# Twelve transposes of the first batch moved from DMA to TensorE, with the whole instruction order laid out anew

## The chip, the cores and the metric

The kernel is one program on one core of a Trainium2 chip. The metric is the time of one execution in microseconds, as the device measures it. The engines are named as the profile names them: PE is TensorE (PEld its weight loads), DVE is VectorE, ACT is ScalarE, POOL is GpSimd, SP is SyncE, which here only issues DMAs.

## The reference

Two things are computed one after the other. First, attention for 8 batches of 8 heads, with 512 local tokens and 32 global tokens of 64 numbers each. A global token looks at all 544 keys; a local token looks at the 32 global keys and at the local keys at most 32 places away. Second, an MLP on all 4,352 resulting tokens:

```python
x = attn_out.transpose(0, 2, 1, 3).reshape(B * S, H * D)     # 4352 x 512
h = x @ w_in                                                  # 512 x 2048
g = np.where(h >= 1, h, np.where(h <= -1, 0.0, (h + 1) ** 2 / 4))
out = (g @ w_out).astype(np.float32)                          # 2048 x 512
```

The two weight matrices arrive as 64-bit floats, 8 MB each.

## The kernel before, in words

Every operand of TensorE is held as two fp16 halves, a high one and a low one that is the difference; a product is three products of halves. The two weight matrices are cut into 16 tiles each. A tile of `w_in` is loaded (step `Lw`), decoded from 64-bit words (`wd`, VectorE for the most part), brought to a common scale that needs eight tiles (`ws`), and split into halves (`wh`); `w_out` goes through `Lo`, `od`, `oh` likewise.

A batch goes through these steps. Keys, queries and values are loaded. `scale_k` finds a scale for the keys; in the first two batches it does so by a Gram matrix on TensorE, 24 products. `prep_k` and `prep_q` split and transpose, `swap_q` exchanges halves by a DMA, `prep_v` splits the values and `prep_w` shifts windows of them by DMAs. For each of four blocks of 128 queries and each of two groups of four heads, `att_q` makes the scores (32 small products), `att_a` the probabilities (VectorE adds the mask and finds the extreme, ScalarE takes the exponential, one engine casts the high half, one subtracts for the low half) and transposes them, `att_b` multiplies them with the values (48 small products). `att_x` divides by the sums (VectorE, tile `small_rc`), casts, subtracts and transposes the block's output. Then the MLP follows in 16 stages of 256 tokens, two to a batch: `moe1` (stages 0 and 1, which are batch 0) or `moe_f` (all later ones) make the hidden values, `act` the activation, `moe2` the output. Two more short MLP stages serve the global tokens.

A transpose of a tile of 128 rows and eight blocks of 128 columns is done by `turn` in one of two ways: as one DMA, which SP issues, or as eight transposes on TensorE into a PSUM bank, which ScalarE or VectorE then copies out:

```python
    def turn(who, o, i):
        if who == "d":
            dma_t(o, i)
            return
        n = i.shape[0]
        t = ps_t.tile([P, 8, P], F16, tag="p", name="turn")
        for c in range(8):
            nc.tensor.transpose(t[:, c, :n], i[:, c * P:(c + 1) * P], ident[:n, :n])
        (nc.scalar.copy if who == "a" else nc.vector.tensor_copy)(o, t[:, :, :n])
```

Which way is taken stands in the string `T["turns"]`, 23 letters for a batch: 6 for keys, 5 for queries, 8 for probabilities, 4 for attention outputs. There are letters for batch 0 alone; every later batch uses the DMA. Other strings of `T` choose engines: `casts` and `subs` for the high and low half of the probabilities, `lows` for the low half of an attention output, `glow` for that of an activation, `queues` the issuing queue of each plain DMA (`s` is SP, `a` is ScalarE).

No scheduler orders the instructions. The functions are recorded first and cut into some 4,400 pieces, each of one engine; the table `ORDER` says in which order the pieces are issued, so it sets each engine's own order, and `SLOTS` says which buffer each tile takes. The semaphores follow from the data and the buffers. Every engine works strictly in its order: a piece that waits holds up all that stand behind it on that engine. Nearly all instructions carry the line of the loop that issues them (L1345, L1348 for DMAs on ScalarE's queue, L1350 for DMAs on SP's), so rows are told apart by their tiles: `room` holds most working tiles, `bank` is PSUM, `weights_w` the weights, `twin` the raw `w_out` and later combined weights, `keys_kt` the transposed keys.

Of the kernel before, what the change touches and what calls it, by code (L numbers as in the profile page):

```python
# [131 lines left out]
def attention_moe(nc, memory, q_l, k_l, v_l, q_g, k_g, v_g, w_in, w_out, out):  # L132
# [1137 lines left out]
    for _, _, fn, a in sorted(steps.values(), key=lambda x: x[:2]):  # L1270
# [8 lines left out]

SLOTS = {  # L1280
# [27 lines left out]
}  # L1308

T = dict(es="nnnn", gramq="aaaaaaaa", dg="vvvvvvaaaaavvav", sid="vvvvv", fast=2, grams="ppaaaaaa", sqs="maamaa", cb=200, cbs=5, lk0=4.19,  # L1310
         lq0=1.76, lv0=12, sk=12, sq=14, subs="pppvpppppvppppvppvpvpvpppvpppvvvppppvvvpppppvppvvppvvpppvppvvvpv",
         glow="vpvpppvpvpppppvvvppppppvvppppvvpvppvvppppvvpppvvpppvpppvppppvpppppppvvpvvpppvvpppppvvvvvpppvvpvvvvpvpvppppvvvpppvvpvvvvvpvvvppvppppppppppppppppp",
         turns="aaaaaaaaaaadddddddddddd", casts="vavavvvaavvvvavvvvvvvvaavaavvaaavvaavaaavaaaavaavvavvaaavvvaavav",
         mags="aapapvpaappvppppppapapaaaaapaaaa", lowx="pppppppvpvpvpvpvppppvpvvpppvpppvpvvvpppppvvppppp",
         lows="vvpvvpppppppppppvppppppppppppppp", halves="aaaaaahaabacadacceccacdbidffcbdf", shifts="vavvaaavvvvaaavvvvvavvvvvaaavvvv",
         splits="wpvpwwpvwwvpvvvw", att=1.35, s0=60, s1=100, s2=254.09, wd0=4, wds=2.06, wd8=19.2, wdt=1.9, wh=1.5, whs=1.4, od=58.2,
         ods=2.2, oh=0.7, ohs=0.92, e0=25.78, e1=70, e2=120, e3=156, w0=24.7, w1=24.34, w2=25.15, w3=25.51, z1=18.29, lq1=24, lv2=24.36,
         sv=24.5, sqb=35.02, pk2=20.4, pk3=30, pk4=45.8, pq2=28.03, pq4=44, pv=35.24, pvs=0.33, lw=0.54, lo=32.46, los=2.12, mk=8, mks=2,
         queues="aaaasaaassaaaaassasaassssssaaasaasaaaaaaaasasaaasssassasssasasaasssassasaasaaaaaassassssaasasaaaasaassaaaaaaaaaaaaaasasassasaaaaasssasasssassassaassssasassaaaaaaasssassasaaaaasaaaasaaasaaasaaassasssasaaasssaaaassaaaassaaasssasaassssaaaassaaaaaaasssssssssasssssaasasaaassaasssaasassaaasssassasasaassasaasaasasssaaaassaasasasasaasssaassssasaaasassasssaassssssaasassasassssasssssasasaaaassaasassasaassssasssasaaasasasasaaasasasasaaasaasaaaasssaassasaaasasasaaaaaasasaaasssaasasaaaassssasassasasaasssaassaasaaasssassasaasssaassaasssssssssasssaassassasasassaaasssasasssasssassasasa")
# [66 lines left out]
```

## Time and profile before

| | |
|---|---|
| median of 3 runs | 975.25 us (972.88 to 977.69) |
| the profiled execution | 969.92 us |
| its span, first to last instruction | 968.1 us |
| PE busy | 849.6 us (88%) |
| DVE busy | 764.6 us (79%) |
| ACT busy | 640.7 us (66%) |
| POOL busy | 312.8 us (32%) |

The span lies 1.8 us under its own execution's time, and that execution lies 5.3 us under the median. Busy shares are means over a start in which little can be computed yet and a long middle in which PE hardly rests, so they are to be read by stretch.

### The profile page before, as it was taken

The numbers are of one execution on the slowest core, as the hardware profiler recorded it, in microseconds if no ns is written. First come the engines' busy times: TensorE is split into PE (matmuls) and PEld (weight loads), VectorE is DVE, ScalarE is ACT, GpSimd is POOL, SyncE is SP. The second block draws the span as 40 slices with busy tenths as digits, with TensorE's granted clock in tenths as the row PEclk, the third lists the DMA queues.
The fourth block names the chain that finished last, engine by engine and source line by source line (L and its number), as shares of the span: only waits on it lengthen the run. The fifth ranks groups of instructions, "written<-read, shape, count | busy, mean of one in ns | idle before, by whom it ended". The sixth has DMA issues, their size and how long they took to land.

```text
span 968.1 us, 34765 instructions
## 1 busy us (share of the span) xinstructions
PE 849.6 (88%) x14284; PEld 608.4 (63%) x14284; DVE 764.6 (79%) x2014; ACT 640.7 (66%) x1581; POOL 312.8 (32%) x343
## 2 busy tenths in 40 slices
PE   0464888998898989998899999999899999999998
PEld 0242675856776675767576757676686677677953
DVE  0788998999788887798788797688899888766861
ACT  1386686869786776677586785768686767455540
POOL 2235345234222422531244320533222324234030
PEclk9996899999999999999999999999999999999999
DMA  9977988899989999898988799978998795755101
GB/s 243 239 145 168 209 162 158 134 181 176 153 148 193 168 173 149 152 168 156 164 148 152 137 166 143 158 152 160 173 160 171 145 162 95 132 81 82 48 1 44
DMA packets 392383, 144.10 MB, mean 149 GB/s; under 512 B 361248, under 2 KB 370464, under 8 KB 392224
## 3 DMA queue, kind: packets, MB, share of 16 engines
q1 hardware_dynamic: 305248, 95.37, 58.2%
q10 hardware_dynamic: 86976, 46.52, 22.9%
q8 instruction: 112, 1.84, 0.8%
q14 instruction: 47, 0.39, 0.2%
HBM read 49.81 MB, written 8.91 MB: 61 GB/s over the span
## 4 chain that ended last, share of the span: by engine, by line
PE 28%; DVE 20%; DMA 16%; ACT 10%; issue 6%; POOL 3%; SPq 2%; ACTq 1%; DVEq 0%; POOLq 0%
PE bank L1345 28%; DVE room L1345 12%; DMA room<-room 11%; ACT room L1345 8%; DVE bank L1345 3%; POOL room L1345 3%; ACT junk_junka L1345 2%; DMA keys_kt<-room 1%; DMA room<-in_v_l_dram 1%; ACTq L1348 1%; DVE batch_small_ms L1345 1%; DMA room<-in_v_g_dram 1%; SPq L1345 1%; SPq L1350 1%; DVE small_nb L1345 1%
## 5 line engine op out<-in xcount | busy, mean ns | idle before, releaser
L1345 POOL TENSOR_TENSOR room<-room,room 128x512 f16<-128x512 f32 (+3 forms) x221 | 244.8, 1120 | 532.1 <-ACT room L1345 407.3
L1345 PEld LDWEIGHTS <-room 128*32 128x32 f16 (+1 forms) x7464 | 241.9, 97 | 244.5 <-issue 38.7
L1345 PE MATMUL bank<-weights_w,room 128*128 128x512 f16 x1632 | 372.9, 381 | 7.1 <-POOL room L1345 2.4
L1345 PEld LDWEIGHTS <-weights_w 128*128 128x128 f16 (+1 forms) x3968 | 222.5, 99 | 63.6 <-DVE weights_w L1345 37.3
L1345 PE MATMUL bank<-room,weights_w 128*128 128x128 f16 (+1 forms) x3840 | 222.8, 217 | 7.4 <-ACT room L1345 3.1
L1345 ACT CAST room<-room 128x512 f16<-128x512 f32 (+1 forms) x238 | 136.1, 586 | 83.5 <-DVE room L1345 59.0
L1345 PE MATMUL bank<-room,twin 128*128 128x128 f16 (+1 forms) x2304 | 131.1, 216 | 12.1 <-DMA room<-room 9.6
L1345 PEld LDWEIGHTS <-twin 128*128 128x128 f16 x2304 | 124.6, 98 | 18.6 <-DMA room<-room 9.0
L1345 ACT ACTIVATE room<-room,small_nb 128x128 f32<-128x128 f32 x256 | 100.4, 394 | 40.8 <-DVE small_nb L1345 25.2
L1345 ACT ACTIVATE room<-bank,batch_small_ms 128x512 f32<-128x512 f32 (+1 forms) x112 | 82.8, 749 | 37.4 <-DVE bank L1345 20.0
L1345 DVE SCALAR_TENSOR_TENSOR bank<-bank,batch_small_ms,room 128x512 f32<-128x512 f32 (+1 forms) x112 | 80.4, 723 | 19.8 <-ACT room L1345 19.5
L1345 ACT ACTIVATE junk_junka<-room 128x512 f16<-128x512 f32 (+2 forms) x124 | 77.5, 625 | 14.0 <-DMA room<-in_k_l_dram 2.8
L1345 DVE TENSOR_TENSOR room<-room,room 128x512 f16<-128x512 f32 (+1 forms) x97 | 75.3, 780 | 10.1 <-ACT room L1345 9.8
L1345 DVE CUSTOM_DVE_ANT_0 room<-bank,const_mask,batch_small_q 128x128 f32<-128x128 f32 x256 | 73.8, 345 | 11.7 <-PE bank L1345 9.8
L1345 DVE SCALAR_TENSOR_TENSOR room<-room,batch_small_ms,bank 128x512 f32<-128x512 f32 (+1 forms) x112 | 79.1, 713 | 1.3
L1345 ACT COPY room<-bank 128x512 f32<-128x512 f32 (+2 forms) x100 | 55.5, 571 | 29.4 <-PE bank L1345 15.0
L1345 DVE SCALAR_TENSOR_TENSOR room<-room,batch_small_ms,room 128x512 f32<-128x512 f32 (+1 forms) x64 | 49.8, 780 | 6.9 <-ACT room L1345 5.1
L1345 DVE TENSOR_TENSOR bank<-bank,room 128x512 f32<-128x512 f32 (+1 forms) x64 | 42.2, 659 | 16.6 <-PE bank L1345 7.2
L1345 PE MATMUL bank<-keys_kt,room 128*32 128x128 f16 x2048 | 40.6, 221 | 10.7 <-DMA room<-room 6.9
L1345 ACT ACTIVATION_READ_ACCUMULATOR room<-room,small_nb 128x1 f32 x256 | 48.6, 190 | 0.0
L1345 PE MATMUL bank<-room,room 128*32 128x64 f16 x3072 | 35.7, 197 | 14.0 <-DMA room<-room 10.5
L1345 PE MATMUL bank<-weights_w 128*128 128x128 bf16 x128 | 15.2, 266 | 35.5 <-DVE weights_w L1345 35.5
(167 smaller groups left out, 916.3 us busy)
## 6 DMA issues: line engine op xcount, KB each, us to landing
room<-room ACTq DMA_DIRECT2D x80, 128.0 KB, 3.7
room<-room SPq DMA_DIRECT2D x64, 128.0 KB, 5.1
weights_w<-in_moe_w_in_dram ACTq DMA_DIRECT2D x25, 256.0 KB, 5.1
twin<-in_moe_w_out_dram ACTq DMA_DIRECT2D x23, 256.0 KB, 5.2
out_dram<-room SPq DMA_DIRECT2D x21, 256.0 KB, 2.9
room<-in_q_l_dram ACTq DMA_DIRECT2D x18, 256.0 KB, 4.2
room<-in_v_l_dram SPq DMA_DIRECT2D x23, 192.0 KB, 4.1
room<-in_k_l_dram ACTq DMA_DIRECT2D x22, 192.0 KB, 5.3
```

Of the source, the lines that this page charges most:

```text
L1345: getattr(getattr(tc.nc, engine), op)(*a, **k)
L1348: tc.nc.scalar.dma_start(*a)
L1350: r = tc.nc.sync.dma_start(*a)
```

## The change

The last twelve letters of `turns` change from `d` to `v` (8 transposes of probabilities) and `a` (4 transposes of attention outputs): in batch 0 these twelve tiles are now transposed by TensorE, and VectorE or ScalarE copies them out of PSUM. The strings `subs`, `glow`, `casts`, `lows`, `lowx` and `queues` hold other letters, and `ORDER` and the large lines of `SLOTS` are other tables of nearly the same length (12 pieces more in `ORDER`). No arithmetic changes.

```diff
-ORDER = ("7 14 5 4 3 16 11 10 17 88 36 40 15 35 152 153 0 1 ...
+ORDER = ("9 8 61 62 63 40 193 64 0 298 66 41 38 39 3 29 27  ...
-    "small.amk": "1 1 0 0 1 0 1 0",
+    "small.amk": "0 0 1 0 1 0 0 1",
-         lq0=1.76, lv0=12, sk=12, sq=14, subs="pppvpppppvppppvppvpvpvpppvpppvvvppppvvvpppppvppvvppvvpppvppvvvpv",
-         glow="vpvpppvpvpppppvvvppppppvvppppvvpvppvvppppvvpppvvpppvpppvppppvpppppppvvpvvpppvvpppppvvvvvpppvvpvvvvpvpvppppvvvpppvvpvvvvvpvvvppvppppppppppppppppp",
-         turns="aaaaaaaaaaadddddddddddd", casts="vavavvvaavvvvavvvvvvvvaavaavvaaavvaavaaavaaaavaavvavvaaavvvaavav",
-         mags="aapapvpaappvppppppapapaaaaapaaaa", lowx="pppppppvpvpvpvpvppppvpvvpppvpppvpvvvpppppvvppppp",
-         lows="vvpvvpppppppppppvppppppppppppppp", halves="aaaaaahaabacadacceccacdbidffcbdf", shifts="vavvaaavvvvaaavvvvvavvvvvaaavvvv",
+         lq0=1.76, lv0=12, sk=12, sq=14, subs="ppppppvppvppvpppppppvpvppvppvppppvvvvvpppvppvppppvpppvvvpppvpvpp",
+         glow="ppppvvpppvpppvppppvvppvppvpvvppvpppppvpvppvpppvvppppvvvppvvpvvvpppvpvvpvppppvppvppvpvpvpppppppvvpvpppppvppppvvvvpvppvpvvpppvppvvpppppppppppppppp",
+         turns="aaaaaaaaaaavvvvvvvvaaaa", casts="aaaaaavvaaaavvvvvvvaavavaaavvvaaavvaaaaaavaavvvvvaaaavvaavavaaav",
+         mags="aapapvpaappvppppppapapaaaaapaaaa", lowx="ppppppppvpvvpppvppppppvpvpppvpvvvppvvpvppppvpvpp",
+         lows="ppppvpppppppvpppppvpvpppvpppvpvp", halves="aaaaaahaabacadacceccacdbidffcbdf", shifts="vavvaaavvvvaaavvvvvavvvvvaaavvvv",
```

VectorE, the first rows of the program. `weights_w_0_69`, `_75`, `_72`, `_67` and `_68` are tiles of `w_in` in decoding; `small_amk` belongs to the scale of the first batch's keys, which lie in `room_94` to `room_99`. Before:

```order
L1345 TENSOR_SCALAR weights_w_0_75<-weights_w_0_75 128x512
L1345 SCALAR_TENSOR_TENSOR bank_123<-bank_123,weights_w_0_75 128x512
L1345 TENSOR_SCALAR room_119<-weights_w_0_72 128x512
L1345 SCALAR_TENSOR_TENSOR weights_w_0_75<-weights_w_0_75,bank_123 128x512
L1345 TENSOR_SCALAR weights_w_0_69<-weights_w_0_69 128x512
L1345 TENSOR_SCALAR weights_w_0_67<-weights_w_0_67 128x512
L1345 SCALAR_TENSOR_TENSOR bank_101<-room_102,weights_w_0_69 128x512
L1345 SCALAR_TENSOR_TENSOR weights_w_0_69<-weights_w_0_69,bank_101 128x512
L1345 SCALAR_TENSOR_TENSOR bank_92<-bank_92,weights_w_0_67 128x512
L1345 SCALAR_TENSOR_TENSOR weights_w_0_67<-weights_w_0_67,bank_92 128x512
```

Now:

```order
L1345 TENSOR_SCALAR weights_w_0_69<-weights_w_0_69 128x512
L1345 SCALAR_TENSOR_TENSOR bank_101<-room_102,weights_w_0_69 128x512
L1345 SCALAR_TENSOR_TENSOR weights_w_0_69<-weights_w_0_69,bank_101 128x512
L1345 MEMSET const_ones_84 128x128
L1345 TENSOR_REDUCE small_amk_106<-bank_107 128x1
L1345 TENSOR_SCALAR small_amk_106<-small_amk_106 128x1 x2
L1345 TENSOR_SCALAR small_dg_108<-const_negid_85,small_amk_106 128x128
L1345 TENSOR_REDUCE small_amk_106<-bank_109 128x1
L1345 TENSOR_SCALAR batch_small_sk_110<-small_amk_106 128x1
L1345 RECIPROCAL batch_small_sk_110<-batch_small_sk_110 128x1
L1345 TENSOR_SCALAR room_155<-room_98,batch_small_sk_110 128x8x64
L1345 TENSOR_SCALAR room_156<-room_99,batch_small_sk_110 96x8x64
```

The scale of the keys stood behind 44 rows, of which the decoding of eight tiles and their common scale; it now stands behind the decoding of one tile and the setting of a constant.

VectorE around the division of the first attention output (the `TENSOR_TENSOR` with `small_rc`). Before:

```order
L1345 CAST room_116<-room_134 128x512
L1345 SCALAR_TENSOR_TENSOR bank_93<-room_133,twin_150 128x512
L1345 TENSOR_SCALAR twin_163<-twin_163 128x512
L1345 TENSOR_SCALAR room_121<-room_98,batch_small_sk_108 128x8x64
L1345 TENSOR_TENSOR room_142<-bank_127,small_rc_158 128x512
L1345 SCALAR_TENSOR_TENSOR room_121<-room_98,batch_small_sk_108,room_121 128x8x64
L1345 TENSOR_SCALAR small_den_157<-small_sum_154 128x8
L1345 TENSOR_SCALAR batch_small_ms_164<-batch_small_ms_164 128x1 x2
L1345 RECIPROCAL batch_small_ms_164<-batch_small_ms_164 128x1
```

Now (a `COPY` of 128x1024 takes transposed probabilities out of a bank):

```order
L1345 COPY room_119<-bank_92 128x1024
L1345 TENSOR_SCALAR twin_157<-twin_157 128x512
L1345 SCALAR_TENSOR_TENSOR bank_92<-room_99,twin_160 128x512
L1345 COPY room_104<-bank_101 128x1024
L1345 COPY room_144<-bank_93 128x1024
L1345 SCALAR_TENSOR_TENSOR weights_w_0_70<-twin_160,bank_92 128x512
L1345 TENSOR_TENSOR room_113<-bank_107,small_rc_162 128x512
L1345 TENSOR_SCALAR twin_150<-twin_150 128x512
L1345 COPY room_99<-bank_92 128x1024
```

Four copies out of PSUM stand ahead of the division now (three are shown), and a fifth behind it.

SP, where batch 0 is transposed. Before:

```order
L1345 DMA_TRANSPOSE room_105<-room_94 128x8x128
L1345 DMA_TRANSPOSE room_125<-room_135 128x8x128
L1350 DMA room_88<-room_112 64x1024
L1350 DMA room_136<-room_118 64x1024
L1350 DMA twin_153<-in_moe_w_out_dram 128x512
L1350 DMA room_119<-room_144 32x1024
L1350 DMA room_119<-room_111 96x1024
L1345 DMA_TRANSPOSE room_125<-room_116 128x8x128
L1345 DMA_TRANSPOSE room_105<-room_126 128x8x128
L1350 DMA qg_qgb_160<-qg_qga_159 64x256
L1345 DMA_TRANSPOSE room_102<-room_104 128x8x128
```

Now, at the same place of the queue:

```order
L1350 DMA room_125<-in_v_g_dram 32x8x64
L1350 DMA twin_160<-in_moe_w_out_dram 128x512
L1350 DMA room_120<-room_133 64x1024
L1350 DMA twin_147<-in_moe_w_out_dram 128x512
L1350 DMA twin_163<-in_moe_w_out_dram 128x512
L1350 DMA room_154<-in_k_l_dram 96x8x64
L1350 DMA room_156<-room_133 32x1024
L1350 DMA room_120<-room_155 64x1024
L1350 DMA room_156<-room_155 96x1024
L1350 DMA room_118<-room_155 64x1024
```

The transposes are gone, and plain DMAs stand closer together.

## Rows read from the trace of the kernel before

**Rows 1.** Windows: length; PE, PEld, DVE, ACT, POOL busy (instructions); clock, DMA, GB/s.
```profile
0.00:52.00 52.00, 13.76 (x84) 9.00 (x85) 20.62 (x50) 14.89 (x26) 11.76 (x37) 1.00 1.12 239
52.00:111.00 59.00, 35.96 (x491) 20.37 (x491) 52.31 (x161) 45.03 (x103) 27.86 (x35) 0.78 0.74 164
111.00:160.00 49.00, 43.08 (x758) 34.22 (x756) 46.17 (x120) 33.20 (x81) 24.34 (x25) 0.96 0.82 175
160.00:260.00 100.00, 90.91 (x1704) 67.89 (x1703) 89.96 (x259) 76.97 (x199) 34.26 (x34) 1.00 0.98 163
260.00:860.00 600.00, 562.10 (x9797) 405.28 (x9795) 493.19 (x1309) 428.68 (x1090) 191.32 (x189) 0.99 0.88 152
860.00:968.10 108.10, 103.80 (x1463) 71.67 (x1459) 62.30 (x121) 41.97 (x87) 23.26 (x26) 1.00 0.26 52
```

**Rows 2.** What TensorE waited for, 0 to 110 us (waits; total us, times, longest).
```profile
PE bank L1345 <- DVE weights_w L1345: 36.5, 8, 18.9
...
PE bank L1345 <- DMA room<-room: 3.1, 1, 3.1
```

**Rows 3.** What VectorE waited for, 0 to 111 us (waits).
```profile
DVE weights_w L1345 <- DMA weights_w<-in_moe_w_in_dram: 22.6, 2, 16.6
DVE small_amk L1345 <- PE bank L1345: 6.5, 2, 6.2
```

**Rows 4.** Busy time from 0 to 100.3 us (windows).
```profile
0.00:100.30 100.30, 41.54 (x419) 24.30 (x420) 62.71 (x172) 51.27 (x113) 35.73 (x68) 0.89 0.91 199
```

**Rows 5.** Timeline of VectorE at the start (start us, us; idle before).
```profile
16.56 0.43 DVE L1345 TENSOR_SCALAR weights_w<-weights_w 128x512 int32<-128x512 int32 x1 [16.56 <-DMA weights_w<-in_moe_w_in_dram]
...
51.25 0.29 DVE L1345 TENSOR_REDUCE small_amk<-bank 128x1 f32<-128x128 f32 x1 [6.17 <-PE bank L1345]
```

**Rows 6.** Timeline of TensorE: Gram matrix of the keys; one turn on TensorE.
```profile
49.03 2.18 PE L1345 MATMUL bank<-room 128*128 128x128 bf16 x24
...
101.80 0.61 PE L1345 MATMUL bank<-const_ident,room 128*128 128x128 f16 x8
```

**Rows 7.** Timeline of 100 to 111 us, from attention output to first hidden product.
```profile
100.32 0.68 DVE L1345 TENSOR_TENSOR room<-bank,small_rc 128x512 f32<-128x512 f32 x1
...
104.24 0.69 DVE L1345 TENSOR_TENSOR room<-room,room 128x512 f16<-128x512 f32 x1 [0.26 <-ACT room L1345]
...
109.91 1.89 PE L1345 MATMUL bank<-room,weights_w 128*128 128x128 f16 x16
```

**Rows 8.** Groups by line and form (busy us, mean ns of one).
```profile
L1345 POOL TENSOR_TENSOR room<-room,room 128x512 f16<-128x512 f32 x150 | 190.3, 1277 | 476.5 <-ACT room L1345 379.4 <-DVE room L1345 46.6 <-issue 18.4
...
L1345 ACT CAST room<-room 128x512 f16<-128x512 f32 x208 | 125.1, 613 | 77.6 <-DVE room L1345 53.8 <-POOL room L1345 4.3 <-issue 3.6
...
L1345 DVE TENSOR_TENSOR room<-room,room 128x512 f16<-128x512 f32 x92 | 71.4, 780 | 10.1 <-ACT room L1345 9.8
...
L1345 DVE TENSOR_TENSOR bank<-bank,room 128x512 f32<-128x512 f32 x56 | 38.7, 692 | 14.6 <-PE bank L1345 5.4 <-ACT junk_junka L1345 4.9 <-ACT room L1345 4.2
...
L1345 DVE CAST room<-room 128x512 f16<-128x512 f32 x34 | 14.7, 440 | 1.9 <-ACT room L1345 1.8
...
L1345 PE MATMUL bank<-const_ident,room 128*128 128x128 f16 x72 | 7.1, 259 | 2.6 <-DVE room L1345 1.8 <-ACT keys_kt L1345 0.7
...
L1345 ACT COPY keys_kt<-bank 128x1024 f16<-128x1024 f16 x5 | 5.0, 1004 | 2.4 <-PE bank L1345 2.4
...
L1345 DVE TENSOR_TENSOR bank<-bank,room 128x256 f32<-128x256 f32 x8 | 3.4, 426 | 2.0 <-PE bank L1345 1.8 <-ACT room L1345 0.2
```

**Rows 9.** DMA issues (KB each, median us from issue to landing).
```profile
room<-room SPq DMA_TRANSPOSE x152, 4.3
```

**Rows 10.** What TensorE waited for, 160 us to the end (waits).
```profile
PE bank L1345 <- DMA room<-room: 23.9, 23, 2.8
```

**Rows 11.** Timeline of TensorE: first and third of three waits before values, batch 1.
```profile
219.50 0.95 PE L1345 MATMUL bank<-room,room 128*32 128x64 f16 x96 [0.80 <-DVE room L1345]
...
238.87 0.55 PE L1345 MATMUL bank<-room,room 128*32 128x64 f16 x48 [0.37 <-DVE room L1345]
```

More of the change, by code (lines that the diff above doesn't have):

```diff
@@ L1318 @@
          sv=24.5, sqb=35.02, pk2=20.4, pk3=30, pk4=45.8, pq2=28.03, pq4=44, pv=35.24, pvs=0.33, lw=0.54, lo=32.46, los=2.12, mk=8, mks=2,
-         queues="aaaasaaassaaaaassasaassssssaaasaasaaaaaaaasasaaasssassasssasasaasssassasaasaaaaaassassssaasasaaaasaassaaaaaaaaaaaaaasasassasaaaaasssasasssassassaassssasassaaaaaaasssassasaaaaasaaaasaaasaaasaaassasssasaaasssaaaassaaaassaaasssasaassssaaaassaaaaaaasssssssssasssssaasasaaassaasssaasassaaasssassasasaassasaasaasasssaaaassaasasasasaasssaassssasaaasassasssaassssssaasassasassssasssssasasaaaassaasassasaassssasssasaaasasasasaaasasasasaaasaasaaaasssaassasaaasasasaaaaaasasaaasssaasasaaaassssasassasasaasssaassaasaaasssassasaasssaassaasssssssssasssaassassasasassaaasssasasssasssassasasa")
+         queues="saasasaaassaassaaaaasassaaaaaaassasaaaasasaasassasasssasssasssasssssasssaasssssssaaaaasassaaaasassssssaaaaaassasaasaassasaasasssssssssaasssassssssasssaasssssassaasaaaasassasasssaasssssaaassasssssaasassaasssaassasssssassasaassasasaasssaaaasasaasasssssasaassaaasssssasasaasaassaaasssasssssaaaasssssaassssssaassaaaasaasasaaaaassssasasssaassassassaassaaaassasaassssssaasasssssasasassaasaaasssaaaassassaasssasssaassassassssasassaasasasasaassaasssassasssssaasasaaaasssaasssssaassasassasaassssaassassasasassaaassssssassasaaaaasssaassasasassasaassssasasassaassssaasasaaasassaasssasass")
 KEYS = 2
```

2 lines of the change are left out of this document (1 added, 1 removed), and 20 rows, old and new, of the table SLOTS.

## Prediction

> **What bounds the kernel now.** I read the windows first [rows 1]. From 260 us to the end TensorE is busy 665.9 of 708.1 us, so that part is nearly all products and can shrink by at most 42.2 us. From 111 to 260 us it is busy 134.0 of 149 us, and VectorE 136.1: the two press together. Before 111 us TensorE is busy only 49.7 us. It is idle for 61.3 us there, over half of the 118.5 us that it rests in the whole span (968.1 less 849.6). The change has its gain there, if anywhere.
>
> Next, what TensorE waits for in that start: 36.5 us for VectorE's decoding of weights, only 3.1 us for a DMA between tiles [rows 2]. So the DMA transposes are hardly ever what it waits for directly; VectorE is. VectorE in turn waits 22.6 us for loads of `w_in` in two waits, and 6.2 us once for the keys' Gram matrix [rows 3]. Its first instruction starts at 16.56 us, and the 6.17 us end at 51.25 us [rows 5]. From 52 to 111 us it is busy 52.3 of 59 us [rows 1]: the engine that sets the pace. [...]
>
> The mark that I follow is the division of batch 0's first block by its sums, at 100.32 us, and the first hidden product behind it, at 109.91 us [rows 7]. Up to 100.3 us VectorE has worked 62.7 us and rested 37.6 us [rows 4].
>
> **The change, part by part.** *VectorE starts sooner (term A).* The new order asks for one weight tile and then all keys, by size 0.5 and 1.5 MB. At 239 GB/s [rows 1] that is 8.4 us of transfer. With the start of the queues and the way to landing (a transpose takes 4.3 us [rows 9], taken for any DMA here) the keys lie there at 11 to 13 us. The Gram matrix takes 2.2 us [rows 6], so VectorE's first reduction of it comes at about 14.5 us, with the 2 us or so of one tile's decoding done before. That leaves some 13 us of rest there, with the round trip through the scale, in place of the three waits of rows 3 and 5, 16.6 + 6.0 + 6.2 = 28.8 us. The other 37.6 - 28.8 = 8.8 us I keep. Against that, more stands ahead of the division: counted in the two orders, 174 VectorE instructions instead of 156. Each at the mean of its kind in this trace, they sum to 72 instead of 63 us; four copies out of PSUM are 4.4 us of the difference (their price is below). So the division comes at 72 + 13 + 8.8 = 94 us, 6 us sooner. The bounds: nothing gained, if the rest that I keep grows by as much, which the loads allow (all matrices and batch 0 are some 12 MB, 50 us at 239 GB/s, in either order); 9 us gained, if half the 8.8 us goes too.
>
> *Twelve turns leave the DMA (term B).* Removed are twelve issues on SP and twelve times 4.3 us to landing. Added are 96 transposes on TensorE. The nearest row has 72 in 7.1 us, 0.10 each; at best eight take 0.61 us [rows 8, 6]. So 7.3 to 9.5 us, in a stretch where TensorE rests 23 of 59 us [rows 1]; that rest hides them, and without it they would cost their full 9.5. Four copies on ScalarE cost 1.0 us each. Eight on VectorE have no row. ScalarE's 1.0 us is one neighbour. VectorE's sums out of PSUM take 0.692 us for 512 numbers and 0.426 for 256 [rows 8], which carried on to 1,024 gives 1.22, the upper bound; a cast of 512 numbers between working tiles takes 0.44, the lower. I take 1.1, since the PSUM rows are nearer in kind: 8.8 us (3.5 to 9.8). [...]
>
> What the copies cost is partly handed back by the letters: for batch 0 VectorE loses three casts (0.44 each) and three low halves of outputs (0.78 each) [rows 8], 3.6 us, so it has 5.2 us more; ScalarE and POOL get that work (0.61 and 1.28 each) and have room, 45.0 and 27.9 of 59 us [rows 1]. In the whole kernel VectorE's casts fall from 34 to 27 and its subtractions of the other kinds by 7, 8.5 us, so its total hardly moves.
>
> On the marked path one turn counts. From the division to the product it is 9.6 us now [rows 7]: the subtraction ends at 104.93, and the turn by DMA, issue and landing, ends just before 109.91, 5.0 us. In its place stand eight transposes (0.6 to 0.8) and one copy (1.0), about 2.2 us with hand-overs. The subtraction moves to POOL, 0.5 us slower. So term B is 2 us, 0 to 3: less if a place in TensorE's strict order comes late. A and B bring the first hidden product to about 102 us, 8 us sooner.
>
> *What is given back (term C).* The two orders have the same 478 VectorE instructions ahead of the last output product of batch 0's first block, but now they sum to 205.7 instead of 200.1 us with the copies. From 111 to 260 us VectorE works 91% of the time [rows 1]; if it is what binds there, 5.6 of the 8 us go. Of TensorE's work, 7.1 us more stands ahead of that point, 5.8 of it transposes; 1.3 us is done early and comes back. If TensorE binds, almost nothing goes. Both are near full, so I take 2 us.
>
> *The long rest (term D).* TensorE waits 23.9 us for DMAs after 160 us, in 23 waits [rows 10]. The new order leaves the kinds of work the same. I counted how much TensorE work stands between a block's scores and its values, where transpose and windows must fit: the least was 11.3 us and is 26.9 us now. That should close three waits in batch 1, 1.5 us in all with the middle one at 0.36 [rows 11]. Between the values of a stage's second block and the first product that needs its transposed differences, the least falls from 12.6 to 11.3 us. So 1 us gained, with 8 us either way: a sixth of the 42.2 us of late rest, since the order is new in each of 14 stages.
>
> The sum goes from this execution's own 969.92 us: less 6, 2 and 1, plus 2, gives 963. That execution lies 5.3 us under the median of the three, so against the median it is **968 us**, 0.75% under 975.25. The last products are as before: outputs alone, one copy, one store.
>
> **The rivals.** *Given back whole:* VectorE binds from 111 to 260 us, and term C is 5.6 us or more, with a weaker A of 3 us. Then 969.9 - 3 - 2 - 1 + 5.6 = 969.5, or 975 against the median: no change. For it speaks that VectorE is fuller than TensorE in that stretch [rows 1]; against it that its total falls off later, where it works 82%. *Slower:* the waits of TensorE for transposes in the later batches grow. They are 23.9 us in 23 waits, 1.0 us each, and products of a stage's second block now stand closer behind its values. If each of the 14 stages waits 1.5 us more, that is 21 us, and 968 becomes 989. It decides from 12 us on: that takes back 7 and adds 5. For it speaks that these waits are the largest kind after 160 us [rows 10], against it that the work between scores and values grew. *TensorE blocked by softmax:* a transpose in its strict order now waits for the POOL subtraction, where formerly SP waited, and the splitting of weights stands behind it. Eight times 1.28 + 0.61 us [rows 8] are 15 us at most; the 61 us of rest at the start hide most. I fold a cost over 8 us into the slower case. *Nothing of A:* loads land in so different an order that VectorE still starts its steady work at 25 us or later; that ends at 974 to 978.
>
> **How the numbers follow.** A run of this kernel can tell about 0.5% from no change, 970.4 to 980.1 us. My forecast (terms near their middle, 956 to 970 by itself) has 0.53; given back whole or nothing of A, 0.22; slower, 0.25. The likeliest gives 968. For 8 in 10 the range must take the whole of the second case and the better half of the third, down to term A at 9 and D at 9 gained (969.9 + 5.3 - 9 - 3 - 9 + 1 = 955, and a little for C): 950 to 986.
>
> **What would show it.** Right: VectorE's first reduction of the keys' Gram matrix at 13 to 17 us, some 33 us of its work done by 51 us instead of 20, the division at 92 to 97 us, the first hidden product at 100 to 104 us, transposes with `const_ident` 168 instead of 72 times, VectorE copies of 128x1024 at about 1.1 us, TensorE's rest before 111 us under 56 us. Wrong: a VectorE wait of over 5 us between 15 and 50 us; VectorE over 95% from 111 to 260 us with TensorE no fuller; waits for DMAs after 160 us over 35 us.

## The result, and the profile after

The changed kernel takes **929.97 us** (median of 4, 926.23 to 936.2) against 976.47 us: a ratio of 0.953 with an interval of 0.946 to 0.960, 46 us faster (976.47 is the median of four runs, one more than the 975.25 of the first table). The forecast was 968 us, with 950 as the low end of its range.

The profiled execution took 927.49 us with a span of 925.8. The windows of the changed kernel, in the stretches of [rows 1] (the last one ends with the span):

```profile
0.00:52.00 52.00, 17.79 (x246) 14.73 (x247) 30.27 (x79) 24.36 (x48) 18.99 (x51) 1.00 1.05 230
52.00:111.00 59.00, 47.32 (x807) 31.59 (x806) 57.02 (x184) 50.82 (x131) 21.54 (x25) 0.91 0.79 199
111.00:160.00 49.00, 45.17 (x901) 40.28 (x888) 47.67 (x100) 41.72 (x78) 27.41 (x25) 1.00 0.92 166
160.00:260.00 100.00, 94.93 (x1568) 67.36 (x1566) 89.40 (x268) 76.58 (x203) 36.42 (x38) 1.00 0.96 159
260.00:860.00 600.00, 579.99 (x10222) 422.50 (x10221) 489.51 (x1327) 429.41 (x1094) 191.96 (x197) 0.99 0.88 152
860.00:925.80 65.80, 61.89 (x674) 38.97 (x670) 30.91 (x55) 20.86 (x42) 13.91 (x15) 1.00 0.09 29
```

Length less PE busy is TensorE's rest. Before 111 us it fell from 61.3 to 45.9 us, from 111 to 260 us from 15.0 to 8.9, and from 260 us on from 42.2 to 23.9. So of 39.8 us less rest (118.5 to 78.7) the start gave 15.4 and the late batches 18.3. PE busy fell by 2.5 us (849.6 to 847.1), though 96 transposes came in; the 39.8 and the 2.5 make the 42.3 us between the two profiled spans, where the medians lie 46 apart. VectorE is no emptier than before between 111 and 260 us (137.1 of 149 us; it was 136.1), and yet TensorE is fuller there. The stretches are cut by time, and the changed kernel is further in its work at 260 us. Cut by work instead, at the first output product of the seventh MLP stage (467.1 us before, 438.1 now), the rest fell from 92.1 to 61.7 us ahead of it and from 22.3 to 13.1 us from there to the last output products.

What TensorE waited for from 0 to 110 us (first two lines) and from 160 us to the end (third), as in [rows 2, 10]:

```profile
PE bank L1345 <- DVE weights_w L1345: 14.8, 6, 10.4
PE bank L1345 <- DMA room<-in_k_l_dram: 14.0, 2, 12.1
...
PE bank L1345 <- DMA room<-room: 14.1, 11, 3.7
```

The decoding of weights holds TensorE up for 14.8 us instead of 36.5; the keys' load is a new wait of 14.0, as they are now TensorE's first work. The late waits for DMAs fell from 23.9 us in 23 to 14.1 in 11.

The timeline at the marks of the prediction, VectorE's first reduction, the division, ScalarE's copy of the turned output, the first hidden product; then two groups by form:

```profile
16.92 0.29 DVE L1345 TENSOR_REDUCE small_amk<-bank 128x1 f32<-128x128 f32 x1 [9.46 <-PE bank L1345]
...
89.97 0.68 DVE L1345 TENSOR_TENSOR room<-bank,small_rc 128x512 f32<-128x512 f32 x1
...
93.69 1.01 ACT L1345 COPY room<-bank 128x1024 f16<-128x1024 f16 x1
...
95.22 0.96 PE L1345 MATMUL bank<-room,weights_w 128*128 128x128 f16 x14
```
```profile
L1345 DVE COPY room<-bank 128x1024 f16<-128x1024 f16 x8 | 5.3, 676 | 0.0
...
L1345 PE MATMUL bank<-const_ident,room 128*128 128x128 f16 x168 | 15.9, 259 | 9.8 <-POOL room L1345 4.0 <-DVE room L1345 3.4 <-DVE weights_w L1345 2.4
```

The division comes at 89.97 instead of 100.32 us, the product 5.3 us behind it instead of 9.6. A copy on VectorE takes 0.68 us. The 96 transposes cost TensorE 15.9 less 7.1, 8.8 us, as forecast, and TensorE waited 9.8 us ahead of all its transposes instead of 2.6 [rows 8].

ScalarE's waits after 111 us, before and after, and the chain that ended last by engine, before and after, show who sets the pace:

```profile
ACT room L1345 <- PE bank L1345: 28.7, 18, 3.4
PE 28%; DVE 20%; DMA 16%; ACT 10%; issue 6%; POOL 3%; SPq 2%; ACTq 1%; DVEq 0%; POOLq 0%
```
```profile
ACT room L1345 <- PE bank L1345: 62.9, 49, 5.0
PE 57%; DVE 15%; DMA 15%; ACT 6%; issue 4%; POOL 2%; SPq 1%; ACTq 1%; DVEq 0%; POOLq 0%
```

An engine that feeds TensorE and now waits for it, 62.9 instead of 28.7 us, is ahead of it. The last chain runs through TensorE's own work for 57% of the span.

### The profile page after: what moved, and what is told of

The parts are those of the page before. It is cut to its first block, busy times and chain, and to the rows that moved or that the text cites. A ratio compares the mean times of both kernels' runs of the same rounds, so it can differ in the third digit from the quotient of the medians.

```text
span 925.8 us, 34962 instructions
## 1 busy us (share of the span) xinstructions
PE 847.1 (92%) x14380; PEld 615.4 (66%) x14380; DVE 744.8 (80%) x2008; ACT 643.8 (70%) x1592; POOL 310.2 (34%) x350
## 4 chain that ended last, share of the span: by engine, by line
PE 57%; DVE 15%; DMA 15%; ACT 6%; issue 4%; POOL 2%; SPq 1%; ACTq 1%; DVEq 0%; POOLq 0%
PE bank L1345 57%; DVE room L1345 8%; DMA room<-room 7%; ACT room L1345 4%; DMA weights_w<-in_moe_w_in_dram 3%; DMA room<-in_k_l_dram 2%; POOL room L1345 2%; DVE bank L1345 2%; DVE weights_w L1345 1%; DMA room<-in_q_l_dram 1%; DMA room<-in_v_l_dram 1%; DMA room<-in_k_g_dram 1%; DVE small_nb L1345 1%; ACTq L1348 1%; ACT junk_junka L1345 1%
## 5 line engine op out<-in xcount | busy, mean ns | idle before, releaser
L1345 PEld LDWEIGHTS <-room 128*32 128x32 f16 (+3 forms) x7560 | 249.2, 97 | 238.0 <-issue 33.0
L1345 PE MATMUL bank<-weights_w,room 128*128 128x512 f16 x1632 | 367.4, 379 | 2.4 <-issue 1.1
L1345 PEld LDWEIGHTS <-weights_w 128*128 128x128 f16 (+1 forms) x3968 | 221.2, 98 | 34.0 <-DVE weights_w L1345 15.5
L1345 ACT CAST room<-room 128x512 f16<-128x512 f32 (+1 forms) x245 | 140.2, 587 | 65.5 <-DVE room L1345 49.9
L1345 PE MATMUL bank<-room,twin 128*128 128x128 f16 (+1 forms) x2304 | 134.2, 218 | 8.4 <-DMA room<-room 5.8
L1345 PEld LDWEIGHTS <-twin 128*128 128x128 f16 x2304 | 127.0, 99 | 15.4 <-DMA room<-room 7.0
L1345 ACT COPY room<-bank 128x512 f32<-128x512 f32 (+2 forms) x104 | 60.1, 585 | 42.1 <-PE bank L1345 39.8
L1345 DVE TENSOR_TENSOR room<-room,room 128x512 f16<-128x512 f32 (+1 forms) x90 | 68.9, 769 | 15.3 <-ACT room L1345 14.9
L1345 DVE SCALAR_TENSOR_TENSOR room<-room,batch_small_ms,bank 128x512 f32<-128x512 f32 (+1 forms) x112 | 78.7, 711 | 1.0
L1345 DVE TENSOR_SCALAR room<-bank,batch_small_ms 128x512 f32<-128x512 f32 x34 | 25.3, 744 | 25.7 <-PE bank L1345 25.1
L1345 DVE SCALAR_TENSOR_TENSOR room<-room,batch_small_sk,room 128x512 f16<-128x512 f32 (+1 forms) x46 | 38.1, 834 | 5.5 <-ACT room L1345 4.4
L1345 PE MATMUL bank<-keys_kt,room 128*32 128x128 f16 x2048 | 38.1, 224 | 3.8 <-DMA room<-room 3.2
```

Source lines behind the costliest of these rows:

```text
L1345: getattr(getattr(tc.nc, engine), op)(*a, **k)
```

## The experiments

The first theories were: **1**, two separate gains, one at the start and one in the late batches; **2**, the early start closes the later waits; **3**, the twelve turns are the gain. Later came **L**, the waits of a stretch belong to its own order, and **F**, the tables (order, buffers, queues, engine letters, turns) fit one another, and any one changed alone loses. Names that begin with a_ are the changed kernel with one thing altered, b_ the kernel before. Medians of the altered kernels are of 6 to 12 runs; the kernel before had 973.7 to 976.6 us beside them. Rest is TensorE's, span less PE busy of the profiled execution. Since the kernel before moved by 3 us from one group of runs to the next, and the changed kernel's interval is 0.946 to 0.960, differences of 5 to 7 us from the changed kernel are not clear of noise.

| kernel | median us | ratio to before (interval) | rest us |
|---|---|---|---|
| before / changed | 976.47 / 929.97 | 0.953 (0.946 to 0.960) | 118.5 / 78.7 |
| start_a_rest_b | 992.88 | 1.018 (1.014 to 1.023) | 130.7 |
| start_b_rest_a | 982.24 | 1.006 (1.003 to 1.009) | 129.5 |
| half_a_rest_b | 974.15 | 1.002 (0.999 to 1.005) | 109.2 |
| half_b_rest_a | 1002.24 | 1.033 (1.028 to 1.038) | 138.6 |
| a_dma_turns | 952.57 | 0.977 (0.973 to 0.981) | 103.3 |
| a_dma_pb | 937.22 | 0.964 (0.958 to 0.969) | 85.9 |
| a_dma_ax | 935.95 | 0.960 (0.955 to 0.964) | 88.7 |
| b_pe_turns | 993.64 | 1.019 (1.014 to 1.024) | 128.2 |
| b_keys_first | 975.2 | 1.000 (0.996 to 1.004) | 120.8 |
| a_queues_b | 953.51 | 0.982 (0.977 to 0.987) | 98.6 |
| a_letters_b | 975.03 | 1.002 (0.999 to 1.005) | 116.9 |
| a_letters_late_b | 956.76 | 0.983 (0.978 to 0.988) | 102.8 |
| b_letters_a | 1025.68 | 1.052 (1.047 to 1.056) | 158.9 |
| a_order_only | 1012.79 | 1.039 (1.034 to 1.044) | 142.7 |
| a_slots_new | 992.45 | 1.020 (1.015 to 1.026) | 127.7 |
| a_room_new | 990.91 | 1.017 (1.011 to 1.022) | 127.8 |
| a_bank_new | 935.17 | 0.959 (0.954 to 0.964) | 83.8 |
| b_slots_new | 1018.55 | 1.044 (1.040 to 1.049) | 156.3 |

**One order spliced to the other.** Engines and queues follow the order in use; the tiles' buffers are kept where they are free.

```diff
# start_a_rest_b, ORDER from its 735th number on, against the changed kernel
-... 499 835 581 801 830 971 572 500 868 582 ...
+... 499 835 581 801 1255 2130 760 613 481 451 ...
```

Expected of start_a_rest_b:

> The first 738 pieces stand as in the changed kernel (all of batch 0's attention, with its engines, queues and TensorE turns), the other 3,673 in the order, engines and queues of the kernel before. Theory 1, two separate gains: only TensorE's shorter rest at the start is kept, about 17 us, so 957 to 962 us against 976 for the kernel before. Theory 2, the early start is what closes the later waits: 930 to 940 us. Theory 3, the twelve turns are the gain: 930 to 940 us as well.

Expected of start_b_rest_a:

> The reverse: the first 845 pieces stand as in the kernel before (batch 0's attention, transposes by DMA), the others in the order, engines and queues of the changed kernel. Theory 1: the later gain of some 22 us is kept, 950 to 957 us. Theory 2: nothing is kept, 972 to 978. Theory 3: 972 to 978. In all cases the seam between the orders may cost a few us.

Measured were 993 and 982 us. The first goes against all three theories; the second, with a few us for the seam, would fit 2 and 3. In start_a_rest_b the start kept its lead: batch 0's last values begin at 125.2 us, in the changed kernel at 126.5, in the one before at 169.5. Then TensorE stands. Its largest waits from 125 to 215 us:

```profile
PE bank L1345 <- ACT room L1345: 9.3, 1, 9.3
PE bank L1345 <- DVE weights_w L1345: 8.4, 2, 7.7
```

The 7.7 us are ahead of the first output product, for VectorE's work on the weights: the old order seems to call for it where the new start has done less of `w_out`. So here the lead was worth nothing, as the order behind it did not use it. A seam is a disturbance of its own, though, and these runs can't tell where the gain was made.

Expected of half_a_rest_b:

> The first 2,434 pieces (through the attention of batch 3, some 460 us) as in the changed kernel, the others in the order, engines and queues of the kernel before. Theory L, each half's waits belong to its own order: TensorE's rest up to there is 30 us shorter in the changed kernel and stays so, 942 to 950 us. Theory S, an order is fitted to what went ahead of it: the seam and what follows cost 10 us or more of that, 955 to 975 us.

Expected of half_b_rest_a:

> The reverse: 2,409 pieces as in the kernel before, then the order, engines and queues of the changed kernel. Theory L: the 10 us that the changed kernel rests less in its second half, 962 to 969 us against 976. Theory S: 974 us or more.

At 974 and 1002 us theory L falls, and S holds both times. In half_a_rest_b TensorE had rested 58.2 us when stage 6's outputs (those of the seventh stage) began (92.1 in the kernel before, 61.7 in the changed one), and 47 us more from there to the last outputs, where the kernel before rests 22.3. Most of it lies in the 200 us behind the seam.

**The turns.**

```diff
# a_dma_turns; a_dma_pb has "aaaaaaaaaaaddddddddaaaa", a_dma_ax "aaaaaaaaaaavvvvvvvvdddd"
-turns="aaaaaaaaaaavvvvvvvvaaaa"
+turns="aaaaaaaaaaadddddddddddd"
# b_pe_turns: the reverse in the kernel before
```

Expected of a_dma_turns:

> The changed kernel with the twelve turns of batch 0 by DMA again, issued where the TensorE transposes stand; all else as in the changed kernel. Theory 1: the turns are a small part; at about 2.5 us more for each on the way to a product, and a few of them waited for, 933 to 942 us. Theory 3: the turns are the gain, 955 us or more. No effect: 928 to 932.

Expected of b_pe_turns:

> The kernel before with the twelve turns on TensorE, at the places where the DMAs were issued, the copies about 1 us later in the order; all else as before. Theory 1: 970 to 978 us, as TensorE waits for VectorE there. Theory 3: 950 us or less. If a transpose in TensorE's strict order holds up work behind it: over 978.

Expected of a_dma_pb:

> The changed kernel with the eight probability turns of batch 0 by DMA and the four attention-output turns on TensorE. With all twelve by DMA it lost 23 us, the largest waits being of 3 to 7.5 us before values (probabilities) and of 3 us before the first hidden product (outputs). If the eight carry the loss: 945 to 952. If the four outputs do: 930 to 938.

Expected of a_dma_ax:

> The changed kernel with the four attention-output turns of batch 0 by DMA and the eight probability turns on TensorE. The eight by DMA cost 7 us and all twelve 23: if the two parts add, 944 to 948 us, that is 4 us for each output turn, as the DMA of 4.3 us stands on the way to the first products; if only both together hurt, 930 to 937.

In the new order the turns on TensorE are worth 22.6 us, between the two forecasts and nearer theory 3 (the DMA turns also needed another buffer for 5 of the 1,209 tiles of `room`). The eight alone are worth 7, the four alone 6, each hardly clear of noise, so the two parts do not add: either one leaves most of the gain. In the old order the same turns cost 17 us, against theory 3. TensorE's largest wait in a_dma_turns from 85 to 180 us (0.2 us in the changed kernel), the two largest in b_pe_turns from 52 to 160 us, and the same two in the kernel before:

```profile
PE bank L1345 <- DMA room<-room: 13.7, 5, 7.5
```
```profile
PE bank L1345 <- DVE room L1345: 9.5, 7, 2.8
PE bank L1345 <- DVE weights_w L1345: 9.3, 6, 3.0
```
```profile
PE bank L1345 <- DVE room L1345: 3.8, 3, 1.8
...
PE bank L1345 <- DVE weights_w L1345: 2.9, 3, 1.2
```

With DMA turns TensorE waits for the DMA before values. With turns on TensorE in an order not laid out for them it stands ahead of transposes and values for VectorE's results (9.5 us instead of 3.8), and waits for VectorE's weights rise with them (9.3 instead of 2.9), it seems because what is behind in its strict order comes late. That is the rival "TensorE blocked by softmax", real in the old order; in the new one the turns gain in spite of the 9.8 us ahead of transposes.

**Term A by itself.**

```diff
# b_keys_first
-ORDER = ("7 14 5 4 3 16 11 10 17 88 36 40 15 35 152 153 ...
+ORDER = ("36 35 40 28 29 30 37 41 27 38 39 31 33 34 32 7 14 5 4 ...
```

Expected of b_keys_first:

> The kernel before with one tile of w_in and then all keys loaded first, and the keys' scale directly behind the decoding of that tile; all else in the old order, with transposes by DMA. Term A of the prediction by itself: VectorE's wait of 6.2 us goes and its work starts sooner, 968 to 972 us against 975. If a part of the new start alone does not fit what stands behind it: 976 us or more.

975.2 us: no gain. But the run holds only part of term A. VectorE's first reduction of the keys comes at 23.1 us (51.3 in the kernel before, 16.9 in the changed one), the division at 97.9 instead of 100.3 us, and the first hidden product at 108.5 instead of 109.9 us. VectorE's largest waits from 0 to 110 us:

```profile
DVE bank L1345 <- ACT bank L1345: 15.5, 1, 15.5
DVE room L1345 <- ACT room L1345: 8.1, 4, 4.4
DVE weights_w L1345 <- DMA weights_w<-in_moe_w_in_dram: 6.5, 2, 4.9
```

The longest waits of [rows 3] are gone and one of 15.5 us has come, in the decoding of the one tile itself. Its second VectorE instruction needs a part that ScalarE makes, and in ScalarE's order nine loads of `w_in` are issued ahead of it, from 8.5 to 18.9 us; the part starts at 20.2 us. The changed kernel begins with a tile whose part POOL makes, and waits 0.5 us there. Starting sooner needs more of the start in another order than the keys and one tile; what an early start by itself would be worth, this run does not show.

**Queues, letters, order.**

```diff
# a_queues_b
-queues="saasasaaassaassaaaaasassaaaaaaas ...
+queues="aaaasaaassaaaaassasaassssssaaasa ...
# a_letters_b (subs, glow, lows and lowx likewise; a_letters_late_b from letter 9 of casts on; b_letters_a the reverse)
-casts="aaaaaavvaaaavvvvvvvaavavaaavvvaaavvaaaaaavaavvvvvaaaavvaavavaaav"
+casts="vavavvvaavvvvavvvvvvvvaavaavvaaavvaavaaavaaaavaavvavvaaavvvaavav"
```

Expected of a_queues_b:

> The changed kernel with the queue letters of the kernel before (253 of 576 plain DMAs change between SP's and ScalarE's queue, each at its place in the order). If the choice of queue carries much of the later gain: 942 us or more. If it is the order of the engines' work: 929 to 936.

Expected of a_letters_b:

> The changed kernel with the engine letters of the kernel before (casts, subtractions and low halves of all batches), turns and order as changed. If the engines' balance carries the gain: 942 us or more; VectorE then has some 8 us more to do in all. If it is the order: 930 to 938.

Expected of a_letters_late_b:

> The changed kernel with the engine letters of the kernel before in batches 1 to 7 alone; batch 0 keeps the new ones. If the shorter rest in the later batches hangs on these letters: 945 to 955 us, and the loss lies after 200 us. If the loss of the run with all letters came from batch 0: 928 to 936.

Expected of b_letters_a:

> The kernel before with the engine letters of the changed kernel, order, queues, buffers and turns as before. If the new letters are better by themselves (VectorE has 8.5 us less to do): 960 to 972 us. Theory F: 985 us or more.

Expected of a_order_only:

> The changed kernel's order and buffers with the letters, queues and DMA turns of the kernel before. If the order holds the gain: under 960 us. If the losses of the three single reversals add up (45, 24 and 23 us): 1,010 to 1,030. Theory F: over 976, that is no gain is left.

Each old table in the new order loses: queues 24 us (by the two strings 293 letters differ, not 253), letters 45. The later batches' letters alone lose 27, and as expected the loss lies behind 200 us: TensorE's rest there is 49.4 us, 25.8 in the changed kernel. The new letters in the old order lose 51, though VectorE has less to do: TensorE waits 40.5 us for DMAs after 260 us there, against 21.2 in the kernel before:

```profile
PE bank L1345 <- DMA room<-room: 40.5, 25, 3.5
```
```profile
PE bank L1345 <- DMA room<-room: 21.2, 21, 2.8
PE bank L1345 <- ACT room L1345: 6.4, 10, 1.4
```

The new order with the old letters, queues and turns takes 1,013 us, slower than either kernel. That is 83 us over the changed kernel, where the three single losses of 24, 45 and 23 us sum to some 91: it lies in the range for losses that add up. So these three losses do nearly add in the new order, but to twice the whole gain. Of what the diff names, the turns, the letters and the order (with its buffers) were tried without the rest, and none was a gain by itself. The new queues in the old order were not run.

**Buffers, a control.**

```diff
# a_slots_new; a_room_new and a_bank_new change one line each; b_slots_new the same in the kernel before
-    "room": "11 12 4 3 6 5 2 1 0 28 34 11 22 13 10 15 ...
+    "room": "11 12 4 3 6 5 2 1 0 28 34 5 22 13 10 15 ...
-    "bank": "4 5 3 0 7 1 2 6 1 2 6 0 1 3 6 4 ...
+    "bank": "4 5 3 0 7 1 2 4 1 2 3 0 1 1 3 2 ...
```

Expected of a_slots_new:

> The changed kernel with its order, engines, queues and turns, only the buffer of each tile in room, bank and twin chosen anew (each tile takes the buffer that has been free longest). A control for the size of a disturbance. Theory F, the tables fit one another so closely that any one changed alone costs 20 us or more, as with queues, letters and turns: 945 us or more. Theory M, only what moves work between engines and queues costs: 926 to 936 us.

Expected of b_slots_new:

> The kernel before with the buffers of room, bank and twin chosen anew by the same rule (the one free longest), nothing else changed. Theory F: the kernel before was fitted to its buffers too and loses 20 us or more, 996 us or more. If only the changed kernel lives on its buffers, so that they are the gain: within 8 us of 976.

Expected of a_room_new:

> The changed kernel with the buffers of room alone chosen anew, the one free longest. If ScalarE's waits for DMAs that still read a buffer are what cost: 970 to 990 us, with some 40 us of such waits after 260 us. If the banks are the cost: 930 to 940.

Expected of a_bank_new:

> The changed kernel with the PSUM banks alone chosen anew by the same rule. If room carries the cost: 930 to 945 us. If the banks do: 965 us or more.

Which buffer a tile takes, with the same order, engines and queues, is worth 62 us in the changed kernel, more than the whole change, and 44 in the kernel before, against this one other rule of choosing. Theory F's forecasts hold for both kernels, but not its "any one": the banks alone cost 5 us, within noise, and `room` alone 61. After 260 us, in a_room_new (ScalarE's waits, then TensorE's), and the same two in the changed kernel:

```profile
ACT room L1345 <- DMA room<-room: 58.8, 23, 8.0
PE bank L1345 <- ACT room L1345: 25.3, 15, 3.5
```
```profile
ACT room L1345 <- DMA room<-room: 7.7, 8, 1.8
PE bank L1345 <- ACT room L1345: 0.3, 1, 0.3
```

ScalarE's casts are the largest group behind these waits (the group by form in a_room_new, whole span, whose idle time is 25.1 us for such DMAs):

```profile
L1345 ACT CAST room<-room 128x512 f16<-128x512 f32 x215 | 129.1, 613 | 79.9 <-DVE room L1345 40.7 <-DMA room<-room 25.1 <-DVE batch_small_q L1345 4.2
```

The input of such a cast is an engine's result and never a DMA's, so it waits for the buffer that it writes: the one free longest by the order is one that a DMA still reads. ScalarE waits for it, and TensorE for ScalarE. In b_slots_new it is the same: ScalarE's waits for such DMAs after 260 us are 36.6 us instead of 12.0, TensorE's for ScalarE 25.8 instead of 6.4. So part of this cost is that the rule is a bad one, which fits any layout ill; the control does not show that a buffer table must be made for its order.

## Why the prediction was wrong

*Terms A and B* were right in kind and too small. VectorE's first reduction came at 16.9 us (13 to 17 forecast), and it rested 23.4 us ahead of the division (21.8), but had worked 66.6 us by then, not 72; 1.7 of that is the four copies at 0.68 instead of 1.1. So A is 10.4 us instead of 6. The other 3.7 of the 5.4 us seem to come of pricing each instruction at the mean of its kind. A's upper bound was put at 9, but by its own terms half of 8.8 on top of 6 is 10.4, which is what came. Of the signs, VectorE's work by 51 us (29.3 us, 33 forecast), the division and the hidden product missed: the last two came sooner than their ranges. From division to product it took 5.3 instead of 9.6 us, so B is 4.3 instead of 2. The first hidden product came at 95.2 us, 14.7 sooner and not 8. For the copy the nearest rows misled me: they are two-input sums in 32 bits, 0.692 us for 512 numbers [rows 8], carried on to 1.22 us for 1,024, and the f16 copy of 1,024 took 0.676 us. Which of the differences between the two counts, no run shows.

Whether A is a thing of its own is not shown: b_keys_first, which has part of it alone, brings the division 2.4 us forward and gains nothing. The 12 MB given for all matrices and batch 0 are too few, since the two matrices have 8 MB each; they bear only on that term's lower bound, and the forecast does not use them.

*The clock* has no term in the forecast. The sum of PE busy times (1 - granted clock) over windows of 5 us, an estimate of what a granted clock under 1.00 costs TensorE, is 11.8 us in the kernel before and 7.1 after. So up to 4.7 us of TensorE's time came back. 3.6 of it lies before 110 us, where the clock from 52 to 111 us is 0.91 instead of 0.78; how much of that reached the end, where TensorE rests besides, is not shown.

*Term C* (2 us given back) had the wrong sign: from 111 to 260 us TensorE rested 6.1 us less, with VectorE as full as ever. My count of VectorE's work ahead of a point priced its sum, and not which of it TensorE waits for. The point with 478 VectorE instructions ahead of it in both orders (by the kernel's order the last output product of batch 0's third block, not its first) comes at 221.9 instead of 237.7 us: the 14.7 us of the first hidden product had become 15.8, and nothing was given back.

*Term D* is the step that failed most: 1 us gained, with 8 either way, "a sixth of the 42.2 us of late rest". It was 18.3 us. The count pointed the right way, for the least TensorE work between a block's scores and its values rose from 11.3 to 26.9 us, but I priced of it only three waits in batch 1, 1.5 us, and found little change behind the second blocks. In the traces, from SP's issue of a probabilities' transpose to the first product with it, the median of the 56 in batches 1 to 7 rose from 7.4 to 10.0 us; the least of a count did not show that. TensorE's waits after 260 us, now:

```profile
PE bank L1345 <- DMA room<-room: 12.5, 9, 3.7
...
PE bank L1345 <- ACT room L1345: 0.3, 1, 0.3
```

Beside the kernel before (21.2 and 6.4 us, shown above) the DMA waits fell by 8.7 us and those for ScalarE, which term D did not look at, by 6.1: 14.8 of the 18.3. The rival "slower" went the other way: DMA waits after 160 us fell to 14.1 us.

*Behind these* lies an assumption that each part of the diff has a gain of its own, and that these add to the whole. The runs show that they do not: in the new kernel queues, letters and turns taken back one at a time cost 24 + 45 + 23 us, twice the gain, and taken back together 83; in the old one the new letters and turns cost 51 and 17. The 46 us are what one joint layout has over another. They can't be shared out among its parts, and the turns that name the change are no gain in the old order.

What stays open: whether another layout with DMA turns would have gained as much; I had no such layout. Which tables made the 18 us of the late batches is not shown either, since each kernel that mixes the two brought waits of its own.

## What to carry to other kernels

Where order, buffers and engine choices were all laid out together, don't price the diff part by part: read from the trace how much rest there is for the new layout to take (here 61 us early, 42 late), and give that a wide range on the side of the gain. A single part copied from such a kernel into another gained nothing here and mostly lost, and one undone tells what that part is worth in that layout only. For a buffer, look at when its last reader ends, a DMA above all: going by how long it has been free in the order cost 61 us here, though no run tried a better rule.

## What the hardware showed that I had not expected

One wait of TensorE cost nearly twice its length. Windows of the changed kernel around a wait of 3.24 us, and the products that end it:

```profile
371.00:374.00 3.00, 2.85 (x48) 2.68 (x48) 3.00 (x8) 2.06 (x6) 0.00 (x0) 1.00 0.99 187
374.00:377.50 3.50, 0.34 (x4) 0.34 (x5) 2.29 (x7) 0.93 (x2) 1.54 (x1) 0.84 1.18 135
377.50:381.00 3.50, 3.50 (x36) 3.50 (x35) 0.00 (x0) 1.06 (x2) 0.00 (x0) 0.50 0.68 167
381.00:385.00 4.00, 4.00 (x56) 4.00 (x54) 0.68 (x2) 1.12 (x3) 1.16 (x1) 0.73 0.36 82
385.00:389.00 4.00, 4.00 (x63) 3.53 (x61) 4.00 (x9) 2.93 (x5) 0.00 (x0) 1.00 0.86 148
```
```profile
377.17 5.09 PE L1345 MATMUL bank<-room,twin 128*128 128x128 f16 x46 [3.24 <-DMA room<-room]
```

Behind the rest the granted clock is 0.50 for the next 3.5 us, and 0.73 over 4 more, with TensorE busy throughout: by estimate 3.5 x 0.5 + 4 x 0.27 = 2.8 us lost on top of the 3.24. The products bear it out: the 72 of this shape from 377.17 to 384.05 us, of which the row shows the first 46, took 6.88 us, and the next 24, to 385.39 us, with the clock at 1.00 again, 1.34 us, a pace at which 72 take 4.0. So the rest, a wait for a DMA, stands ahead of 2.9 us of slower work in this trace. A rest of 1.98 us in the same trace, also for a DMA, left the clock at 1.00:

```profile
445.69 1.52 PE L1345 MATMUL bank<-keys_kt,room 128*32 128x128 f16 x96 [1.98 <-DMA room<-room]
...
445.70:450.00 4.30, 4.30 (x136) 2.90 (x137) 4.22 (x15) 1.67 (x3) 1.38 (x1) 1.00 1.30 167
```

So an altered kernel can lose more than it rests, as one here did: b_pe_turns has 9.7 us more rest than the kernel before, but its span is 23.5 us longer; the same sum over windows of 5 us is 23.1 us there instead of 11.8.
